# Attention to an MLP on one core: first product reassociated, scores transposed at birth, Silu with 1/beta in w_out, attention woven into the MLP

## Chip, cores and metric

One core of a Trainium2 chip. The metric is the device time of one execution in microseconds (us); most executions of a kernel agree within 0.3%. TensorE is called PE, VectorE DVE, ScalarE ACT, GpSimd POOL. PEld is PE's weight load.

## The reference

Two attentions in a row over 32 packed queries per head, then an MLP with the gate `h * sigmoid(beta h)`:

```python
# q, k, v: (8 batches, 8 heads, 576, 64)   p: (8, 8, 32, 64)
P   = softmax(p @ k.T / 8) @ v            # 32 packed rows per head
out = softmax(q @ P.T / 8) @ P            # A2 @ P
x   = out.transpose(0, 2, 1, 3).reshape(4608, 512)
h   = x @ w_in                            # 512 -> 2048
g   = h * (1 / (1 + exp(-beta * h)))      # beta per column of h
y   = g @ w_out                           # 2048 -> 512, f32
```

## The kernel before

It runs in two stages. Attention goes by groups of four heads, two groups side by side, and fills a resident `xT`; the MLP then goes over nine blocks of 512 tokens. Scores of the second attention are born with tokens on partitions, normalised there, and transposed back chunk by chunk. The code is cut (`# ...`).

```python
def _attn_quad(...):
    # ... k, v, q arrive in 256 B runs, are cast on ACT, transposed on PE, exp, P (p_pack)
    for c, sz in enumerate(SIZES):                    # 128 tokens each
        s2ps = ps_sc.tile([128, 128], f32, ...)
        # ... 4 small matmuls: scores of 4 heads
        nc.scalar.activation(e2t[0:sz, :], s2ps[0:sz, :], EXP, scale=SCALE)
        nc.vector.tensor_reduce(z2[0:sz, :], ...)     # row sums, reciprocal, spread: 3 DVE steps
        nc.vector.tensor_tensor(a2t[0:sz, :], e2t[0:sz, :], rz2e[0:sz, :], MULT)
        _tp(nc, a2c_ps[:, 0:sz], a2t[0:sz, :], identr[:sz, :sz])
        nc.vector.tensor_copy(A2_sb[:, 128 * c : 128 * c + sz], a2c_ps[:, 0:sz])
    for pi in range(2):
        # ... OU_ps = p_pack.T @ A2 (x, transposed), 8 matmuls on 32x64 tiles
        nc.scalar.copy(xT[:, 2 * m + pi, b * S : (b + 1) * S], OU_ps[:, :])

def _mlp_block(...):
    for ft in range(16):
        for kt in range(4):                           # contract 512
            _mm(nc, h_ps[:], w_in_bf[:, kt, ...], xT[:, kt, ...], ...)
        nc.scalar.activation(th[:], h_ps[:], TANH, scale=beta_half[:, ft : ft + 1])
        nc.vector.scalar_tensor_tensor(g_all[:, ft, :], th[:], 1.0, h_ps[:], ADD, MULT)
    # ... 4 x 16 matmuls o_ps = g.T @ w_out, out = 0.5 * o_ps
```

The softmax here doesn't subtract the row's maximum and nothing guards it: scores larger than these inputs give would overflow.

## Time and profile before

| | us | where it is read |
|---|---|---|
| time, median | 526.19 (525.47 to 527.4) | its first three runs |
| attention | 269 | first matmul of h_ps |
| MLP | 249 | 18 blocks of 13.81 in the chain |
| PE, ACT, DVE busy | 424, 255, 218 | busy totals |

The main views are shown and read in the prediction below. One more belongs here, because two of the change's parts aim at it. These are rows of the costliest groups: line, engine, operation, output and inputs, count, then busy us and mean ns of one, then the idle time before them and what ended it.

```profile
L254 DVE SCALAR_TENSOR_TENSOR g_all<-th,h_ps 128x512 bf16<-128x512 bf16 x144 | 99.0, 687 | 142.0 <-ACT th L253 142.0
L38 PE MATMUL h_ps<-xT,w_in_bf 128*128 128x512 bf16 x576 | 128.5, 384 | 0.0
L38 PE MATMUL o_ps<-w_out_bf,g_all 128*128 128x512 bf16 x576 | 125.8, 379 | 0.0
L253 ACT ACTIVATE th<-h_ps,beta_half 128x512 bf16<-128x512 f32 x144 | 98.9, 687 | 28.1 <-PE h_ps L38 28.1
```

The gate costs ACT and DVE 0.69 us each per block of 512 columns, while PE needs 4 x 0.216 = 0.86 us to make the block. So Silu in place of Tanh and a DVE step saves busy time that was hidden; by these figures it would not move the MLP stage by itself.

### The profile page before, as it was taken

Reading aid. Unit: us, or ns where it says so; the run is one execution under the profiler, and the core shown is the slowest. Engines: PE = TensorE matmul, PEld = TensorE weight load, DVE = VectorE, ACT = ScalarE, POOL = GpSimd, SP = SyncE. Lnnn points to the kernel's source line nnn. Section 1 sums busy time; section 2 is a strip of 40 time slices with the busy share of each in tenths; the row PEclk is TensorE's granted clock in tenths of the full one; section 3 lists DMA queues with packets and bytes.
Section 4 is the critical chain, followed back from the end, with each engine's and each line's share of the span. In section 5 each row is a group of like instructions: output and inputs, shape, how many; then the busy total and the mean of one; then the engine's idle time right before and its main releaser. Section 6 shows DMA issues by size and latency. Waiting matters only on the chain.

```text
span 525.3 us, 7290 instructions
## 1 busy us (share of the span) xinstructions
PE 423.9 (81%) x2608; PEld 210.9 (40%) x2608; DVE 217.7 (41%) x722; ACT 254.6 (48%) x517; POOL 18.1 (3%) x26
## 2 busy tenths in 40 slices
PE   0175387868676686667689999999999999999997
PEld 0043154434344353433424444444444444444443
DVE  0047055563726255371637070716253433425260
ACT  1344456556473635637237271727363545445361
POOL 3312300000000000000000000000000000000000
PEclk9999999999999999999999999999999999999999
DMA  8997888888875360000000101010111101010102
GB/s 257 301 210 191 242 190 186 181 194 190 186 171 117 87 149 1 2 1 0 1 1 2 60 21 60 21 58 23 40 42 41 41 20 61 21 61 21 60 1 80
DMA packets 126900, 47.15 MB, mean 90 GB/s; under 512 B 119696, under 2 KB 119696, under 8 KB 126352
## 3 DMA queue, kind: packets, MB, share of 16 engines
q1 hardware_dynamic: 121920, 38.29, 29.1%
q10 hardware_dynamic: 4944, 8.40, 4.7%
q8 instruction: 20, 0.33, 0.3%
q14 instruction: 16, 0.13, 0.1%
HBM read 37.23 MB, written 9.44 MB: 89 GB/s over the span
## 4 chain that ended last, share of the span: by engine, by line
PE 59%; issue 12%; ACT 10%; DVE 7%; DMA 7%; SPq 3%; POOL 1%; ACTq 0%
PE h_ps L38 24%; PE o_ps L38 24%; DMA wout<-in_moe_w_out_dram 4%; SPq L63 3%; PE OU_ps L38 3%; DMA v_quad<-in_v_dram 2%; ACT kT_p L86 2%; DVE z L202 2%; PE kT_ps L44 2%; DVE A_sb L219 2%; PE a2c_ps L44 2%; ACT k_bf L71 2%; DVE rz2e L211 1%; ACT xT L235 1%; PE E1T_ps L44 1%
## 5 line engine op out<-in xcount | busy, mean ns | idle before, releaser
L254 DVE SCALAR_TENSOR_TENSOR g_all<-th,h_ps 128x512 bf16<-128x512 bf16 x144 | 99.0, 687 | 142.0 <-ACT th L253 142.0
L38 PE MATMUL h_ps<-xT,w_in_bf 128*128 128x512 bf16 x576 | 128.5, 384 | 0.0
L38 PE MATMUL o_ps<-w_out_bf,g_all 128*128 128x512 bf16 x576 | 125.8, 379 | 0.0
L253 ACT ACTIVATE th<-h_ps,beta_half 128x512 bf16<-128x512 f32 x144 | 98.9, 687 | 28.1 <-PE h_ps L38 28.1
L38 PEld LDWEIGHTS <-w_in_bf 128*128 128x128 bf16 x576 | 56.5, 99 | 69.8 <-issue 3.4
L38 PEld LDWEIGHTS <-g_all 128*128 128x128 bf16 x576 | 56.4, 98 | 67.9
L266 ACT ACTIVATE o_sb<-o_ps 128x512 f32<-128x512 f32 x36 | 21.5, 597 | 102.5 <-PE o_ps L38 102.5
L200 ACT ACTIVATE e2t<-s_ps 128x128 bf16<-128x128 f32 (+1 forms) x80 | 19.8, 273 | 87.6 <-issue 51.4
L44 PE MATMUL kT_ps<-identr,k_bf 128*128 128x128 bf16 (+1 forms) x160 | 24.6, 291 | 40.7 <-ACT k_bf L71 33.1
L38 PE MATMUL OU_ps<-A_sb,p_pack 32*64 32x64 bf16 (+1 forms) x128 | 29.2, 431 | 11.7 <-ACT xT L235 8.4
L44 PE MATMUL a2c_ps<-identr,a2t 128*128 128x128 bf16 (+1 forms) x80 | 19.5, 277 | 22.2 <-DVE a2t L216 21.4
L44 PEld LDWEIGHTS <-k_bf 128*128 128x128 bf16 (+1 forms) x160 | 14.3, 123 | 54.4 <-ACT k_bf L71 36.5
L128 DVE TENSOR_TENSOR Z<-Z1a,Z1b 128x1 f32<-128x1 f32 x16 | 2.4, 151 | 70.3 <-ACT E_sb L126 70.3
L159 DVE COPY qT_h<-qT_ps 64x576 bf16<-64x576 bf16 x64 | 29.1, 454 | 5.3 <-PE qT_ps L44 4.0
L38 PE MATMUL Pun_ps<-v_bf,E1T_sb 128*32 128x64 bf16 (+1 forms) x320 | 31.2, 238 | 0.0
L235 ACT CAST xT<-OU_ps 128x576 bf16<-128x576 f32 x32 | 20.4, 639 | 22.0 <-PE OU_ps L38 22.0
L44 PE MATMUL qT_ps<-identr,q_bf 128*128 128x128 bf16 (+1 forms) x160 | 23.6, 292 | 5.4 <-ACT q_bf L134 5.4
L38 PE MATMUL s_ps<-p_packT,qT_h 64*128 64x32 bf16 (+1 forms) x320 | 20.7, 191 | 6.7 <-ACT e2t L200 3.9
L38 PEld LDWEIGHTS <-E1T_sb 128*32 128x32 bf16 (+1 forms) x320 | 20.2, 113 | 9.9
L44 PEld LDWEIGHTS <-a2t 128*128 128x128 bf16 (+1 forms) x80 | 8.3, 103 | 38.9 <-DVE a2t L216 30.0
L38 PEld LDWEIGHTS <-qT_h 64*128 64x128 bf16 (+1 forms) x320 | 17.0, 110 | 14.5 <-issue 8.3
L86 ACT COPY kT_p<-kT_ps 128x576 bf16<-128x576 bf16 x32 | 19.8, 642 | 5.4 <-POOL w_out_bf L306 2.8
(44 smaller groups left out, 295.6 us busy)
## 6 DMA issues: line engine op xcount, KB each, us to landing
out_dram<-o_sb SPq DMA_DIRECT2D x36, 256.0 KB, 2.0
k_quad<-in_k_dram SPq DMA_DIRECT2D x64, 128.0 KB, 2.8
v_quad<-in_v_dram SPq DMA_DIRECT2D x64, 128.0 KB, 2.8
q_quad<-in_q_dram SPq DMA_DIRECT2D x64, 128.0 KB, 2.8
win<-in_moe_w_in_dram ACTq DMA_DIRECT2D x4, 1024.0 KB, 6.8
wout<-in_moe_w_out_dram ACTq DMA_DIRECT2D x16, 256.0 KB, 3.5
k_quad<-in_k_dram SPq DMA_DIRECT2D x16, 64.0 KB, 3.1
v_quad<-in_v_dram SPq DMA_DIRECT2D x16, 64.0 KB, 2.7
```

Source lines behind the costliest of these rows:

```text
L38: return nc.tensor.matmul(out, lhsT, rhs, start=start, stop=stop, tile_position=tile_position, skip_group_check=True)
L44: return nc.tensor.matmul(out, in_, ident, is_transpose=True, tile_position=tile_position, skip_group_check=True)
L63: nc.sync.dma_start(dst[0:sz, c, :].rearrange("p (h d) -> p h d", d=D), src[b, h4, 128 * c : 128 * c + sz, :].rearrange("h p d -> p h d"),)
L71: nc.scalar.copy(tbf[:, 0:4, :], t32[:, 0:4, :])
L86: nc.scalar.copy(tsb[:], tps[:])
L159: nc.vector.tensor_copy(qh[:, :], tps[64 * li : 64 * li + 64, :])
L200: nc.scalar.activation(e2t[0:sz, :], s2ps[0:sz, :], EXP, scale=SCALE)
L202: nc.vector.tensor_reduce(z2[0:sz, :], e2t[0:sz, :].rearrange("p (h j) -> p h j", j=NP), axis=mybir.AxisListType.X, op=ADD,)
L235: nc.scalar.copy(xT[:, 2 * m + pi, b * S : (b + 1) * S], OU_ps[:, :])
L253: nc.scalar.activation(th[:], h_ps[:], TANH, scale=beta_half[:, ft : ft + 1])
L254: nc.vector.scalar_tensor_tensor(g_all[:, ft, :], th[:], 1.0, h_ps[:], ADD, MULT)
L266: nc.scalar.mul(o_sb[:], o_ps[:], 0.5)
```

## The change

The intent is to give PE fewer columns and no pauses:

- **Reassociation.** `(A2 @ P) @ w_in = A2 @ (P @ w_in)`. Per batch, W = P @ w_in has 8 heads x 32 = 256 rows, so h contracts 256, not 512.
- **Transposed scores.** Scores are computed with keys on partitions; sums over keys become matmuls with ones. No transpose of weights is left.
- **Silu.** `h * sigmoid(beta h) = silu(beta h) / beta`: beta is multiplied into W, 1/beta into w_out.
- **Loads.** Token 4p+t lies on partition p, so a partition reads 4 tokens, 1 KB at a time.
- **Weaving.** One loop over batches; phase i holds the first product of batch i, the attention of batch i+1 and the second product of batch i-1, in a hand-set order.

The kernel is written anew; this is its core, cut.

```diff
+    def fused_w(self, b, n):                       # W = P @ w_in, 512 columns at a time
+        for c in range(NC):
+            for r in range(2):
+                self.mm(ps[32*c:32*c+32, r, :], pp[64*r:64*r+64, c, :],
+                        self.w_in_bf[64*r:64*r+64, c, cols], pos=(64*r, 32*c))
+        self.nc.vector.tensor_tensor(W[:, :, cols], ps, beta_bc[:, cols]..., ALU.mult)
+    def mlp_main(self, b, ft):
+        for r in range(2):                         # contract 256 in place of 512
+            self.mm(ps[:], W[:, r, 128*ft:128*ft+128], A[:, r, 0:SM], start=(r == 0), stop=(r == 1))
+        self.nc.scalar.activation(self.g[b][:, ft, :], ps[:], AF.Silu)
+    def cast_w_out(self, n, t):
+        for i in range(4):
+            self.nc.gpsimd.tensor_scalar_mul(self.w_out_bf[:, ft, :], t[:, i, :], self.rbeta[:, ft:ft+1])
+    def run(self):                                 # ... batch 0: load, attention, W, with w_in by quarters
+        o2 = self.load_w_out(2); self.cast_w_out(1, o1)      # two staging buffers for w_in and w_out
+        o3 = self.load_w_out(3); self.cast_w_out(2, o2); self.cast_w_out(3, o3)
+        for x in "kqv": self.load(1, x)
+        for x in "kqv": self.cast(1, x, pcopy)     # pcopy: POOL
+        # ... loads of batch 2
+        for i in range(B): self.phase(i)
+    def phase(self, i):                            # main(ft, n): h of one ft, then n matmuls of second(i-1)
+        main(0, 2); attn("transpose_main", nb, "k"); main(1, 2); attn("transpose_main", nb, "q")
+        # ...
+        attn("exp_set"); attn("scores1", nb); attn("silu_set"); fill(14)
+        main(6, 2); attn("packed", nb)
+        # ...
+        attn("exp_set"); attn("scores2", nb); fill(8); attn("norm2", nb); attn("silu_set"); fill(8)
+        # ... fused_w 0 to 3 among main 10 to 15, remainder of 64 tokens, rest of second(i-1)
```

## The prediction

> **What bounds the kernel now.** I read the page first: busy totals and the 40 slices. They show a kernel in two halves.
>
> ```profile
> span 525.3 us, 7290 instructions
> PE 423.9 (81%) x2608; PEld 210.9 (40%) x2608; DVE 217.7 (41%) x722; ACT 254.6 (48%) x517; POOL 18.1 (3%) x26
> PE   0175387868676686667689999999999999999997
> DVE  0047055563726255371637070716253433425260
> ACT  1344456556473635637237271727363545445361
> DMA  8997888888875360000000101010111101010102
> ...
> PE 59%; issue 12%; ACT 10%; DVE 7%; DMA 7%; SPq 3%; POOL 1%; ACTq 0%
> ```
>
> From about slice 21 on (13 us each) PE is full. Before it no engine is: attention has PE, DVE and ACT at 4 to 8 tenths, and DMA full only for 13 slices. The chain of waits says the same: the matmuls of h_ps and o_ps carry 24% each, and the rest is a ladder of small pieces on every engine. Busy time by stretch puts the border near 269 us (columns: stretch, length, busy us and instructions of PE, PEld, DVE, ACT, POOL, then clock, DMA share, GB/s):
>
> ```profile
> 0.00:40.00 40.00, 12.70 (x114) 7.76 (x114) 6.61 (x22) 13.53 (x29) 10.72 (x14) 1.00 0.93 255
> 40.00:200.00 160.00, 110.56 (x948) 63.49 (x945) 78.76 (x386) 85.34 (x219) 7.34 (x12) 1.00 0.73 170
> 200.00:269.00 69.00, 47.94 (x391) 26.41 (x389) 33.38 (x170) 33.50 (x88) 0.00 (x0) 1.00 0.00 1
> ```
>
> Even at 200:269, where DMA is idle, PE is busy 69%: attention is bound by latency between engines, not by data. The second half is bound by PE issue: in the chain in order of time every 64 matmuls of 512 columns take 13.81 us, 216 ns each, 18 such blocks = 249 us.
>
> The timeline gives what small matmuls cost:
>
> ```profile
> 300.68 13.81 PE h_ps L38 x64
> 314.49 13.81 PE o_ps L38 x64
> ...
> 181.60 1.48 PE L44 MATMUL kT_ps<-identr,k_bf 128*128 128x128 bf16 x10 [2.13 <-ACT k_bf L71]
> 183.21 0.45 PE L38 MATMUL S1a_ps<-kT_p,pT_p 64*32 64x320 bf16 x4
> 183.81 0.40 PE L38 MATMUL S1b_ps<-kT_p,pT_p 64*32 64x256 bf16 x4
> ```
>
> Four matmuls on four 64x32 tiles of the array take 0.45 us together, where one lasts 0.453 us: they run at the same time. In the starts of single instructions the full-height transposes follow each other in 107 ns, and each change to a 64-row one and back adds about 0.25 us.
>
> **What the Trainium skill says.** "TensorE: Matmul & The Clock Gate", Part 3 (Packing small matmuls): matmuls on different row and column tiles run concurrently; the S1a row agrees. "TensorEngine Tiling (Array Packing)", Key Properties: changing the tiling mode drains the engine; the 0.25 us agrees in kind. "ScalarE: Activation LUTs", What ACT_TABLE_LOAD costs: 1283 ns, plus a drain of 1380 ns, per switch to another set. The trace has one load, 1283 ns, with the next ACT instruction starting right at its end, so I count 1.3 us and keep the drain as a risk. "DMA: Bandwidth & Descriptors", Why small descriptors are slow: small ones waste the engines. Here 119,696 of 126,900 packets are under 512 B; the busy first 20 us moved 269 GB/s with the weights' large rows among them, the next stretches 183 to 227 at 81 to 88% share.
>
> **The change, part by part.** Per batch of 576 tokens:
>
> (1) First product. Before: 576 matmuls of 512 columns, 124 us, plus A2@P (OU_ps, 29 us busy) and its copies (xT, 20 us of ACT). After: W = P@w_in costs 4 groups of 8 tiled matmuls (64x32, 512 columns); if all 8 run at once a group is 0.22 us plus 0.25 us of mode change. Then h = A2@W contracts 256 rather than 512: 32 matmuls = 6.9 us, and 32 of 64 columns for the remainder, about 1 us at 30 ns. So 8 x (6.9 + 1.0 + 1.9) = 78 us in place of over 124.
>
> (2) Second product: 36 tiles x 16 x 0.216 = 124 us, unchanged. This is the floor that remains.
>
> (3) Scores born transposed: E1T and a2c transposes (80 matmuls each), the row sums, the rz2e copies and 320 + 320 small matmuls go. Left per batch: 36 transposes of 107 ns = 3.9 us; scores1 0.6; packed 1.2; scores2 0.3; norm2 0.5; two more mode changes 0.5. About 7 us.
>
> (4) Weaving. Attention for batch b+1 is laid in program order among the MLP matmuls of b and the second product of b-1. PE per phase: main 6.9 + remainder 1.0 + W 1.9 + attention 7.0 + second product 13.8 (4 tiles) or 17.3 (5 tiles) = 30.6 or 34.1.
>
> (5) ACT per phase: 18 Silu at about 0.60 (the row o_sb, 128x512 from PSUM with an immediate scale, took 597 ns; Tanh with a pointer scale 687) = 10.8; Exp and Ln 6.3 (about 0.2 + 0.85 ns per column, from 597 ns at 512 and 1045 at 1024); 4 table loads 5.1. Sum 22, below PE. DVE: 2 copies of 2048 bf16 (425 ns at 512, 223 at 128, so 1.2 each), 4 products of 1024 f32 (687 at 512, so 1.2 each), A2 1.3, outputs 2.7, the rest 1.5: 13. POOL: 3 casts at about 2.1 (1892 ns at 2048) = 6.4. DMA: 3.5 MB of load and 1.2 MB of store in over 30 us, with 1 KB runs: idle two thirds of the time. So PE alone binds, and this time in all stages.
>
> I walked one phase in program order to see where PE waits. Table load after the sixth Silu at 9.4 us, Exp until 12.3, Silu table back at 13.6; PE meets packed at 13.4 and main 8 at 15.8, both just ready. Second switch 17.7 to 19.0, E2 ready at 20.3, where the fill of 8 has just run out at 20.1; Ln and Exp run under 14 fills. Sum 32.3 or 35.8: 1.7 us of small waits over the pure PE sum.
>
> (6) Ends. At the start nothing overlaps: k, p, v, q and the first quarter of w_in are 5.1 MB, 21 us at 0.27 MB/us. Then the first attention and the quarters of w_in alternate: only two staging buffers, so quarter 3 is issued after quarter 1 is cast; W is complete at about 40 us. w_out goes through the same two buffers until about 53 us with scaling on POOL to 55; the loads of batch 1 stand behind it in the queue and land to 63 us, and their casts stand behind on POOL. Phase 0 needs those, starts late and has no second product to fill with: Silu at 0.6 and four table loads bind, some 20 us after q arrives. Phase 0 ends at about 85 us. Phase 7 has no attention: 6.9 + 1.0 + 13.8 = 22. Then 80 bare matmuls 17.3, copy and store 3.2.
>
> Sum: 85 + 3 x 32.3 + 3 x 35.8 + 22 + 20.5 = 332; 4 us for cold-clock stretches and semaphores I did not see: **336 us**.
>
> **Rivals.** (a) Table switching binds: with the 1.38 us drain, each pair of switches delays Silu and Exp by 2.8 us where fills run out; 3 to 5 us in 7 phases, so 355 to 370. For it: the page. Against: the trace's one load shows no gap behind it, and fills of 14 and 8 cover much. (b) The tiled groups of 8 do not run all at once (two row groups on one column group were seen only as a pair on different columns): 4 at once costs 0.2 us x 5 groups x 8 = 9 us; fully serial 1.5 x 5 x 8 = 60 us, near 395. Against serial: the S1a row. (c) The start is worse: single-buffered loads, small staging, f32 matmuls for beta, slow strided casts on POOL: plus 10 to 20 us. Or better, if 1 KB runs reach 0.33 MB/us: minus 8. (d) Nothing gained because PE was 81% busy already: the 424 us count overlapping latencies (384 ns for a matmul issued every 216), so busy is no measure of work; I give this no weight.
>
> **Range and chances.** Start plus or minus 12, phases minus 1 to plus 4 each, tail firm: 318 to 360. To be slower than 516 us, everything would have to fail together. Faster by over 2%: 0.98; within 2%: 0.01; slower: 0.01.
>
> **What would show it.** Right: from 85 us on PE at 9 tenths in nearly every slice; second product still 216 ns a matmul; phases of 32 and 36 us by turns; W groups of 8 in under 0.6 us; ACT 45 to 60% busy; DMA at 1 to 3 tenths. Wrong: PE gaps of over 1 us before packed, main 8 or z2 in each phase, released by ACT (rival a); W groups over 1 us (b); first output-product matmul after 100 us (c). An ACT or POOL busier than PE would make the whole sum wrong.

## The result, and the profile after

The changed kernel takes 333.15 us (332.07 to 334.49, four runs) against 526.14 us of the kernel before in its runs beside it; the ratio is 0.633 (95% interval 0.631 to 0.635). The output is correct.

First the page: busy totals, the 40 slices (8.3 us each; PEclk is the clock recorded for PE in tenths of full, DMA the busy share of the 16 DMA engines) and the chain of waits by engine.

```profile
span 331.5 us, 5201 instructions
PE 257.6 (78%) x2188; PEld 134.7 (41%) x2225; DVE 120.4 (36%) x155; ACT 167.7 (51%) x242; POOL 77.4 (23%) x69
PE   0297320006659999999999999999999999999994
ACT  1024230000986877587458757862886687443300
POOL 3030008999520520440043005200510000000000
PEclk9999555555969999999999999999999999999999
DMA  8960553599994492097029606912010010111122
...
PE 71%; ACT 7%; POOL 7%; DMA 5%; issue 4%; DVE 4%; DVEq 0%; POOLq 0%
```

PE is full from the thirteenth slice to the end, in one stage now rather than in half the kernel. The other thing to see is the front: PE at zero in the seventh to ninth slice while POOL stands at 8 to 9 tenths.

The busy time by phase says how long each part is. The stretches begin at the first h matmul of each batch; the first two lines are the start, then phases 0, 1, 2, 7 and the tail. Phases 3 and 5 repeat phase 1, phases 4 and 6 repeat phase 2.

```profile
0.00:49.10 49.10, 19.73 (x184) 15.94 (x185) 21.75 (x34) 11.80 (x14) 6.23 (x11) 0.82 0.61 184
49.10:77.50 28.40, 1.09 (x11) 0.17 (x4) 1.23 (x1) 0.60 (x1) 26.58 (x18) 0.50 0.73 229
77.50:103.90 26.40, 19.46 (x196) 10.51 (x200) 10.31 (x12) 19.18 (x29) 11.33 (x11) 0.77 1.08 288
103.90:132.90 29.00, 28.14 (x260) 14.31 (x265) 12.80 (x16) 20.70 (x30) 6.66 (x6) 1.00 0.54 152
132.90:165.20 32.30, 31.33 (x279) 15.71 (x281) 13.46 (x17) 21.36 (x31) 6.66 (x6) 1.00 0.51 151
...
287.80:309.40 21.60, 21.50 (x126) 10.26 (x127) 2.98 (x5) 10.15 (x17) 0.00 (x0) 1.00 0.15 49
309.40:331.50 22.10, 17.38 (x86) 7.80 (x84) 3.94 (x6) 0.60 (x1) 0.00 (x0) 1.00 0.21 72
```

Set these beside the sum of the prediction:

| part | predicted | measured | difference |
|---|---|---|---|
| start and phase 0 | 85 | 103.9 | +18.9 |
| phases 1 to 6 | 3 x 32.3 + 3 x 35.8 = 204.3 | 3 x 29.0 + 3 x 32.3 = 183.9 | -20.4 |
| phase 7 | 22 | 21.6 | -0.4 |
| tail | 20.5 | 22.1 | +1.6 |
| not seen | 4 | | -4 |
| sum | 336 | 331.5 (span) | -4.5 |

So the total came out by luck: two of its terms were off by some 20 us in opposite directions. The experiments ask for the cause of both, and what the large gain is made of.

The late start, in the timeline (start us, length us, instructions, then the idle time before and what ended it):

```profile
50.92 24.65 POOL L412 TENSOR_SCALAR w_out_bf<-w_out,rbeta 128x512 bf16<-128x512 f32 x16 [31.05 <-DMA w_out<-in_moe_w_out_dram]
75.52 1.89 POOL L87 CAST k_bf<-k 128x2048 bf16<-128x2048 f32 x1
77.47 1.89 PE L63 MATMUL kT_ps<-identr,k_bf 128*128 128x128 bf16 x16 [27.30 <-POOL k_bf L87]
```

POOL scales w_out for 24.65 us without a pause, casts k of batch 1 behind it, and PE, idle for 27.30 us, transposes k the moment that cast ends. One scaling lasts 24.7 / 16 = 1.56 us (1563 ns on the page). The same tile's plain cast in the kernel before took 0.61 us, and the prediction's end at 55 us fits that length.

The short phases, in the timeline of PE in phase 2:

```profile
133.67 1.06 PE L63 MATMUL kT_ps<-identr,k_bf 128*128 128x128 bf16 x16
...
147.88 0.44 PE L58 MATMUL s_ps<-qT,pp 64*32 64x512 bf16 x16
148.48 1.68 PE L58 MATMUL o_ps<-w_out_bf,g_main 128*128 128x512 bf16 x7 [0.16 <-issue]
150.76 0.65 PE L58 MATMUL z_ps<-E2T,bones 128*128 128x512 bf16 x4 [0.60 <-ACT E2T L212]
...
153.06 0.41 PE L58 MATMUL w_ps<-w_in_bf,pp 64*32 64x512 bf16 x8
```

Sixteen transposes take 1.06 us from first start to last end; in the single records they start 56 ns apart, where the same instruction at 77.47 takes 107. Eight tiled matmuls of 512 columns end within 0.41 us: all eight run at once. The only waits of PE that the timeline lists in this phase are the two shown, 0.16 and 0.60 us.

### The profile page after: what moved, and what is told of

It reads as the page before. It is cut to its first block, busy times and chain, and to the rows that moved or that the text cites. A ratio compares the mean times of both kernels' runs of the same rounds, so it can differ in the third digit from the quotient of the medians.

```text
span 331.5 us, 5201 instructions
## 1 busy us (share of the span) xinstructions
PE 257.6 (78%) x2188; PEld 134.7 (41%) x2225; DVE 120.4 (36%) x155; ACT 167.7 (51%) x242; POOL 77.4 (23%) x69
## 3 DMA queue, kind: packets, MB, share of 16 engines
q1 hardware_dynamic: 47488, 46.15, 46.8%
## 4 chain that ended last, share of the span: by engine, by line
PE 71%; ACT 7%; POOL 7%; DMA 5%; issue 4%; DVE 4%; DVEq 0%; POOLq 0%
PE o_ps L58 34%; PE h_ps L58 18%; POOL w_out_bf L412 7%; PE w_ps L58 4%; DMA p<-in_p_dram 3%; PE kT_ps L63 3%; PE qT_ps L63 3%; PE pp_ps L58 3%; ACT E2T L212 2%; PE brow_ps L58 2%; ACT g_main L266 2%; DMA w_out<-in_moe_w_out_dram 2%; PE z_ps L58 1%; DVE w_in_bf L400 1%; PE s_ps L58 1%
## 5 line engine op out<-in xcount | busy, mean ns | idle before, releaser
L58 PE MATMUL o_ps<-w_out_bf,g_main 128*128 128x512 bf16 x496 | 131.7, 380 | 1.7 <-issue 0.5
L266 ACT ACTIVATE g_main<-h_ps 128x512 bf16<-128x512 f32 x128 | 75.8, 597 | 99.3 <-PE h_ps L58 89.5
L58 PE MATMUL h_ps<-A2T,W_bf 128*128 128x64 bf16 (+1 forms) x494 | 83.7, 288 | 1.2 <-ACT g_main L266 0.7
L58 PEld LDWEIGHTS <-g_main 128*128 128x128 bf16 x512 | 47.9, 98 | 55.6 <-issue 2.7
L303 DVE COPY o_sb<-o_ps 128x512 f32<-128x512 f32 x36 | 24.9, 692 | 103.8 <-PE o_ps L58 103.8
L58 PEld LDWEIGHTS <-W_bf 128*128 128x128 bf16 x512 | 31.1, 98 | 28.3 <-issue 8.3
L249 DVE TENSOR_TENSOR W_bf<-w_ps,beta_bc 128x1024 bf16<-128x1024 f32 x32 | 38.4, 1221 | 10.0 <-PE w_ps L58 9.1
L412 POOL TENSOR_SCALAR w_out_bf<-w_out,rbeta 128x512 bf16<-128x512 f32 x16 | 24.7, 1563 | 31.1 <-DMA w_out<-in_moe_w_out_dram 31.1
L58 PE MATMUL w_ps<-w_in_bf,pp 64*32 64x512 bf16 x256 | 14.6, 434 | 11.7 <-DVE w_in_bf L400 10.7
L126 ACT ACT_TABLE_LOAD x15 | 19.2, 1283 | 4.8 <-issue 4.6
L129 ACT ACT_TABLE_LOAD x15 | 19.2, 1283 | 0.3
L87 POOL CAST q_bf<-q 128x2048 bf16<-128x2048 f32 x8 | 15.1, 1894 | 15.1 <-DMA q<-in_q_dram 15.1
L87 POOL CAST v_bf<-v 128x2048 bf16<-128x2048 f32 x7 | 13.3, 1893 | 20.3 <-issue 18.5
```

The source lines that it names most:

```text
L58: return self.nc.tensor.matmul(out, lhsT, rhs, start=start, stop=stop, tile_position=pos, skip_group_check=True)
L87: copy(o[:, 0:2048].rearrange("p (t h d) -> p h t d", t=4, h=8), t[:, 0:2048].rearrange("p (h t d) -> p h t d", h=8, t=4),)
L126: self.nc.scalar.preload_act_table_set(EXP_SET)
L129: self.nc.scalar.preload_act_table_set(SILU_SET)
L249: self.nc.vector.tensor_tensor(W[:, :, cols], ps, self.beta_bc[:, cols].unsqueeze(1).to_broadcast([128, 2, 512]), ALU.mult,)
L266: self.nc.scalar.activation(self.g[b][:, ft, :], ps[:], AF.Silu)
```

## The experiments

Eleven kernels were run. Those timed over three rounds have four runs, all fast; the others are one look each, of unknown state, and are used only for differences of many per cent or for their traces. All are correct but two.

**1. Is the scaling on POOL what holds the start? (e_cast_only)** The factor is left out, so the result is wrong.

```diff
-            self.nc.gpsimd.tensor_scalar_mul(self.w_out_bf[:, ft, :], t[:, i, :], self.rbeta[:, ft : ft + 1])
+            self.nc.gpsimd.tensor_copy(self.w_out_bf[:, ft, :], t[:, i, :])
```

> The 1/beta factor is left out of w_out on purpose (wrong result): the 16 GpSimd multiplications become plain casts. Theory 1 (the late start is the GpSimd scaling, 16 x 1563 ns in front of the casts of batch 1): the casts take about 0.61 us each, the staging buffers come free sooner, the k cast of batch 1 starts near 66 us instead of 75.5, the total falls by 8 to 12 us to about 323; phases 1 to 6 stay 29.0 and 32.3 us. Rival (the transfers of w_out and of batch 1 bind, GpSimd only looks busy): the k cast moves by under 3 us and the total stays over 330.

Measured: 324.94 us (323.80 to 325.49), 8.2 us less. POOL's timeline in this kernel:

```profile
50.54 2.30 POOL L412 CAST w_out_bf<-w_out 128x512 bf16<-128x512 f32 x4 [30.50 <-DMA w_out<-in_moe_w_out_dram]
...
62.01 2.30 POOL L412 CAST w_out_bf<-w_out 128x512 bf16<-128x512 f32 x4 [1.58 <-DMA w_out<-in_moe_w_out_dram]
65.97 1.90 POOL L87 CAST k_bf<-k 128x2048 bf16<-128x2048 f32 x1 [1.66 <-DMA k<-in_k_dram]
```

Four casts take 2.30 us where four scalings took 4 x 1.56 = 6.2, the k cast starts at 65.97 instead of 75.52, and now it waits for DMA: the engine is no longer the limit, the place of the load in the queue is. Phases 1 to 6 keep their 29.0 and 32.3 us. Theory 1 holds, but it is worth 8.2 of the 18.9 us by which the start was late: without the scaling w_out is still ready only at 64.3 us.

**2. Does the start need w_out at all? (e_order)** Batch 1 is loaded and cast ahead of the second half of w_in and of w_out. w_out is first read in phase 1.

```diff
         self.fused_w(0, 0)
         self.scores2(0)
+        for x in "kqv": self.load(1, x)
+        for x in "kqv": self.cast(1, x, pcopy)
         w2 = self.load_w_in(2)
 # ...
         self.cast_w_out(3, o3)
-        for x in "kqv": self.load(1, x)
-        for x in "kqv": self.cast(1, x, pcopy)
```

> Batch 1 is loaded and cast before quarters 2 and 3 of w_in and before w_out; nothing else changes. Theory 1 (phase 0 waits only for its place in the DMA queue and on GpSimd): phase 0 starts at about 50 us instead of 77 with no wait, phase 1 starts near 77 to 80, when the last w_out part has been scaled; total about 308 (303 to 314). Rival (the DMA engines are the limit of the start): w_in is pushed back by what batch 1 moves, about 12 us, phase 0 starts near 61 and the total is about 320 or more.

Measured: 308.06 us (307.73 to 309.30), correct, ratio to the kernel before 0.585 (0.583 to 0.587). It beats both kernels. The stretch of phase 0 in this kernel:

```profile
51.00:78.60 27.60, 21.11 (x197) 10.69 (x193) 11.60 (x13) 19.56 (x29) 25.96 (x17) 0.81 0.72 222
```

POOL still spends its 25 us on w_out, but beside phase 0, not ahead of it. From the first Silu of a phase to that of the next, phase 0 fell from 54.3 to 27.8 us; W came 1.9 us later and phase 1 grew by 0.7 because batch 2 is cast late. The sum, -26.6 + 1.9 + 0.7 = -24.0, is the change of the span. So an order, in the DMA queue and on POOL, was worth more than the whole first difference of the table.

**3. Do the table loads cost? (e_one_table)** Silu becomes Exp (wrong), so that one table set serves.

```diff
-        self.nc.scalar.activation(self.g[b][:, ft, :], ps[:], AF.Silu)
+        self.nc.scalar.activation(self.g[b][:, ft, :], ps[:], AF.Exp)
     def silu_set(self):
-        self.nc.scalar.preload_act_table_set(SILU_SET)
+        pass                       # and exp_set only once
```

> Silu is replaced by Exp on purpose (wrong result), so that one table set serves all: 29 of 30 table loads of 1.28 us go, all else stays. Theory (loads hide behind PE work except in phase 0): phases 1 to 6 shorten by at most 0.7 us each, the wait of z_ps for E2T, phase 0 by 3 to 5; total 324 to 329. Rival (table switching binds each phase): phases shorten by 2.6 us or more each, total 315 or less.

Measured: 326.13 us (325.10 to 326.49), 7.0 less. Phases 1 to 6 shorten by 0.76 us each, a little more than the 0.7 allowed for; phase 0, where nothing fills, by 2.8. Removing four loads of 1.28 us per phase thus returns 0.76 of 5.1 us: the rest is hidden behind other work. Rival (a) of the prediction falls. The loads show no drain either: in the trace of the changed kernel a load that follows a Silu directly starts 17 or 18 ns after its end, and Exp 11 or 12 ns after the end of the load.

**4. What is the weave worth? (e_unwoven)** The same instructions, with the attention of the next batch as one block behind the MLP.

```diff
-        main(0, 2); attn("transpose_main", nb, "k"); main(1, 2); ...
+        for ft in range(16): main(ft, 4)
+        self.mlp_rem(i, 0); self.mlp_rem(i, 1)
+        for _ in w2: pass
+        attn("transpose_main", nb, "k"); attn("transpose_main", nb, "q"); ...   # all of attention
```

> The attention of the next batch stands as one block behind the MLP of the phase instead of among its matmuls; same instructions. Theory (weaving hides a latency chain of some 18 us of which only 7 us is PE work): phases 1 to 6 grow by about 11 us each to 40 and 43, phase 0 gains some 5, total about 395 (375 to 410), and the transposes fall back to about 107 ns each where PE was idle before. Rival (the fewer and larger instructions carry the gain and order matters little): total within 15 us of 333.

Measured: 399.62 us, 66.5 more. Phases that took 29.0 and 32.3 take 40.9 and 44.4. One long phase:

```profile
137.10:181.50 44.40, 35.65 (x285) 17.85 (x281) 13.61 (x18) 18.20 (x28) 6.60 (x6) 0.85 0.39 111
```

The clock column is 0.85: within each phase the trace has the clock at half for 10 to 14 us (130.8 to 141.1, 171.8 to 185.4). One detail of the expectation missed: the transposes kept 56 ns. They come right behind the dense second product, where the record still says full clock; what ran slow was the W groups at the end of the latency chain and the first matmuls of the next phase. So the weave is worth two things at once, hidden latency and a clock that stays up (1.00 in the woven phases 1 to 7); how the 66.5 us divides between them was not measured.

**5. What is the reassociation worth? (e_noreassoc)** x = A2 @ P is formed again and h contracts 512; beta then goes into w_in once, at its cast on VectorE, and all else stays.

```diff
-    # fused_w: W = P @ w_in, 4 groups of 8 tiled matmuls, times beta
+    # one transpose of P, then per 128 rows of x:
+            self.mm(ps[h, lo:hi], ppT[k, h], A[k, r, lo:hi], pos=(32 * c, 64 * r))
+            self.nc.vector.tensor_copy(xT[:, c, :], ps[:, 0:S])
-        for r in range(2):
+        for r in range(4):        # mlp_main and mlp_rem over w_in * beta and xT
```

> The reassociation alone is undone: x = A2@P is formed per batch (8 tiled matmuls of 512 and 8 of 64 columns, 4 copies of 576 columns on VectorE) and h contracts 512 again, with beta folded into w_in once; weaving, transposed scores, Silu and loads stay. Theory (phases are bound by PE issue): per phase 32 more matmuls of 512 at 0.216 = +6.9, 32 more of 64 columns = +0.9, W groups -1.7, x +1.5, so phases 1 to 6 go from 29.0 and 32.3 to about 36.6 and 39.9; phase 7 +7.8, phase 0 +4; total about 390 (380 to 400). Rival (forming W per batch costs as many matmuls as it saves): within 15 us of 333.

Measured: 386.18 us, 53.0 more. Phases take 36.0 and 39.45, so 7.0 and 7.1 more, against 7.6 expected; 32 more matmuls at 0.216 are 6.9 of it. Phases are bound by PE issue, and the rival falls.

**6. Do the two gains add? (e_both_undone)** Both edits at once.

> Reassociation and weaving both undone (h contracts 512 over x; attention as one block behind each MLP phase). Theory (the two gains are independent: fewer PE columns, and latency hidden): they add, 333 + 53 + 66 = 452 (442 to 462); the 75 us that are left to 526 belong to the rest: scores born transposed, larger instructions, one pass. Rival (they overlap, a longer MLP hides more): under 435.

Measured: 459.63 us. They add nearly: 53.0 + 66.5 would make 452.6, and 7 more was found. The gain of 193 us divides so:

| step | us |
|---|---|
| before to both undone: transposed scores, larger instructions, one loop | 526.9 to 459.6 = 67 |
| reassociation (unwoven, or woven) | 60 or 53 |
| weaving (over x, or over W) | 73 or 66 |

Three of these totals are single; the steps are far above the 0.3% within which most runs agree. The first row was not divided further: what the transposed scores, Silu, the single loop and the clock each carry in it is not shown.

**7. Do the 1 KB runs matter? (e_rows256)** Back to one token per partition row, 256 B at a time.

```diff
-        nc.sync.dma_start(..., src[b, :, 0:SM, :].rearrange("h (p t) d -> p h (t d)", p=128))
+        for i in range(4):
+            nc.sync.dma_start(..., src[b, :, 128 * i : 128 * i + 128, :].rearrange("h p d -> p h d"))
-                rows = ... .rearrange("(p t) n -> p t n", t=4)
+                rows = ... .rearrange("(t p) n -> p t n", t=4)
```

> The 4 tokens per partition are undone: k, v and q come in runs of 256 B (4 DMAs per tensor in place of 1), the output rows follow. Theory (loads are hidden in phases 1 to 6 and GpSimd binds the start): phases 1 to 6 stay 29.0 and 32.3 us, the start is 4 to 8 us later because q of batch 0 and the casts of batch 1 come later; total 337 to 342. Rival (the longer runs carry a large part of the gain, DMA becomes the limit): phases 1 to 4 grow, total over 350.

Measured: 333.96 us (332.33 to 334.20), the same; the expected 4 to 8 us did not come. The packets changed, first the changed kernel's line and then this one's:

```profile
DMA packets 49607, 47.01 MB, mean 142 GB/s; under 512 B 16288, under 2 KB 40880, under 8 KB 49584
```

```profile
DMA packets 124488, 47.02 MB, mean 142 GB/s; under 512 B 115744, under 2 KB 115760, under 8 KB 124464
```

Two things cancelled what I had expected. p landed earlier, so its cast began at 7.2 us and not at 10.5, and batch 1 waited for POOL in both kernels (first cast of k at 73.8 and 75.5). This part of the change carries nothing in the total here. The waste of small packets is real but hidden: for the same 46.15 MB the main queue takes 63.0% of the 16 engines' span instead of 46.8%.

**8. Is 107 ns the transpose, or the clock? (e_order_warm)** In e_order PE waits while W groups 2 and 3 of batch 0 become ready. Useless matmuls fill that wait.

```diff
         ps = self.att("w_ps")...
+        if b == 0 and n >= 2:
+            for _ in range(16 if n == 2 else 12):
+                self.mm(ps[:, 0, :], self.identr[:], dummy)      # 512 columns, overwritten after
```

> The version with batch 1 loaded before w_out, and in it 28 useless matmuls of 512 columns in front of the W groups 2 and 3 of batch 0, where PE waits anyway. Theory (the 107 ns of a transpose is the array at half clock after idling, not a property of transposes or of the instruction mix): the 16 k transposes of phase 0 follow each other in 56 ns rather than 107, the first h matmuls in 216 rather than 427, total 2 to 3 us below the same version without them (308). Rival (transposes are slow unless embedded in other work, or the useless matmuls delay W): 107 ns stays, total the same or up to 3 us more.

Measured: 308.44 us (307.61 to 309.39), so nothing gained on 308.06. But the transposes of phase 0 answer the question:

```profile
52.56 0.60 PE L58 MATMUL h_ps<-A2T,W_bf 128*128 128x512 bf16 x2
53.01 1.06 PE L63 MATMUL kT_ps<-identr,k_bf 128*128 128x128 bf16 x16
```

1.06 us for the sixteen, where the same row reads 1.91 in e_order and 1.89 in the changed kernel. The cause is the clock: it is recorded as full from 48.0 to 61.7 us here, and as half from 31.6 to 82.8 us in the changed kernel, whose sixteen start at 77.47. The time was not saved because the useless matmuls, the first of them at half clock themselves, held W back by as much: phase 0 took 1.8 us less and began 1.1 us later, and phase 1 then waited 0.8 us longer for POOL.

**9. The same question in the kernel before (e_before_3banks, e_before_warm).** The control frees a PSUM bank; the second run adds 576 useless matmuls, each fed by data of its own step so that the scheduler cannot pull them forward.

```diff
-    name="ps_b1", bufs=4, space=PSUM
+    name="ps_b1", bufs=3, space=PSUM
+    # e_before_warm only, at every step of _attn_quad:
+        _mm(nc, fill[:, 0:w], identr[:], src, start=True, stop=True)    # 36 per group of four heads
```

> Control: the kernel before with 3 instead of 4 rotating PSUM tiles in attention, one bank freed. All theories: attention ends 0 to 15 us later than 269 us, the MLP is unchanged, total 526 to 545; transposes still 107 ns apart.

> The control, with 36 useless matmuls per group of four heads (9,216 columns) spread over the attention stage: 61 us more PE issue time at full clock, 123 at half clock. Theory (attention of the kernel before runs on an array at half clock because PE pauses too often, though the record of granted clock says 1.00): transposes follow each other in 56 ns in most of the stage, the first h matmuls in 216 ns, and the useless work costs little: total within minus 25 to plus 25 us of the control. Rival (107 ns is what a transpose costs amid tiled matmuls): 107 ns stays and the total grows by 50 us or more.

Measured: the control 528.20 us, attention ending at 271 us; with the useless work 553.41, attention ending at 298. Of 92 pairs of neighbouring k transposes that the control's trace holds, 60 start 106 to 107 ns apart and none 56; with the useless work 39 of 94 start 55 to 56 ns apart, 11 more 63 to 67, and 37 still 106 to 107, and every h matmul runs at 216 from the first.

The record of the clock agrees: all 39 lie where it says full, and of the 37 slow ones 27 lie where it says half and 10 ahead of its first entry. So the pace follows the clock in this kernel too. But only 105 of the stage's 298 us are recorded at full clock, not most of it, and the total grew by 25.2 us, just outside the range that the theory allowed. Filling with useless work does not pay here; the weave fills with useful work. What the half clock cost the kernel before stays open.

**10. A further step (e_order_head).** On top of e_order_warm, the f32 matmuls that spread beta and the cast of k are issued ahead of the preparation of p.

```diff
-        self.prepare_p(); self.prepare_beta(); w = self.load_w_in(0); self.cast(0, "k", vcopy)
+        self.prepare_beta(); self.cast(0, "k", vcopy); self.prepare_p(); w = self.load_w_in(0)
```

> As e_order_warm, and the beta rows and the cast of k are issued before the preparation of p, so that 7 us of f32 matmuls run while the data is still on its way. Theory (the f32 matmuls stand on the path of the start): scores1 of batch 0 starts 4 to 5 us sooner than 28.9 us and phase 0 as well; total about 301 (299 to 304). Rival (the arrival of q and w_in binds the start): under 2 us of gain over e_order_warm.

Measured: 305.80 us (304.24 to 307.28), correct, ratio 0.580 (0.578 to 0.583): the fastest, 2.6 us below e_order_warm where 7 were expected. scores1 did start 3.8 us sooner than in e_order_warm, at 24.9 us, and the first W group 4.6 us sooner, at 32.8. But the second cast of w_in then took 2.7 us where it takes 1.2 in e_order_warm, with POOL casting v at the same time; the first useless matmuls took 6.5 instead of 5.9 us; and phase 1 lost 0.6 us to late casts. Neither theory had the size.

## Why the prediction was right or wrong

**What bounds the kernel before:** right that the MLP is PE issue; that attention is latency fits, but it missed that attention ran at half clock, and no run separates the two there. It took the clock column, 1.00, as it stood. The clock record in the trace has only one change before the end: to full, at 275.4 us. Before it nothing is recorded, and the page fills the gap with full speed. The timeline shows the change:

```profile
269.04 1.89 PE L38 MATMUL h_ps<-xT,w_in_bf 128*128 128x512 bf16 x4
...
271.47 2.31 PE L38 MATMUL h_ps<-xT,w_in_bf 128*128 128x512 bf16 x5
```

Four matmuls in 1.89 us and five in 2.31. In the single records they start 0.427 us apart, against 0.216 from 275.5 us on. Experiments 8 and 9 show that the 107 ns between k transposes have the same reason.

**Part (1), first product:** right. h took 32 x 0.216 and the remainder about 0.9; a W group costs about 0.44 us with its change of tiling mode (153.06 to 153.41, and 0.09 ahead of it), so 1.7 per phase against 1.9. Undoing it cost 7.0 to 7.1 us per phase.

**Part (2), second product unchanged:** right. Phases with five output tiles are 3.3 us longer than those with four, 16 x 0.216 = 3.45.

**Part (3), "36 transposes of 107 ns = 3.9 us":** wrong size. They take 36 x 0.056 = 2.0. The mechanism, PE issue time of attention, was right; the term was read off an array at half clock. This is 1.9 of the 3.3 us by which each phase was over-estimated.

**Part (4) and the walk:** right in kind, wrong in size. PE is idle for under 1 us per phase (29.00 - 28.14, 32.30 - 31.33), not 1.7, and the one wait of note, z2 behind Exp, was named. Of the 3.3 us, 1.9 are the transposes, about 0.8 the waits and 0.2 the W groups; some 0.4 us per phase remain that I did not assign.

**Part (5), other engines:** ACT 20.3 to 21.4 against 22, DVE 13 against 13, POOL 6.66 against 6.4: right. DMA "idle two thirds of the time" was wrong for phases 1 to 4, where its share is 0.51 to 0.56; it binds in none of these phases, where PE is idle for under 1 us.

**Part (6), "with scaling on POOL to 55":** the step that failed. Its end fits 16 scalings at the 0.61 us of a cast; they took 1.56 each, to 75.6 us, and e_cast_only shows that this cost 8.2 us. W was also complete at about 49 and not at 40 us, which set w_out and batch 1 back as well. The f32 matmuls for beta, unsized in the prediction, took 7.2 us on PE; but having them earlier (e_order_head) brought the first h matmul only 2.6 us forward, so the cause of these 9 us is shown only in part. The chain itself, w_out ahead of batch 1 in the queue and on POOL, was named, and e_order shows that it held phase 0: with the order changed, phase 0 runs as soon as W is complete.

**The rivals:** (a) table switching and (b) serial tiles fell. (c) a worse start came true in size, nearly at the upper end of its 10 to 20 us, and its sign, the first output-product matmul after 100 us, was seen; of its causes the casts on POOL took 1.89 us, as long as expected, and what held the start was the order and the scaling, which it does not list.

**That the total came so close was luck.** With the phases at their measured length the forecast would have been 336 - 20.4 = 316 us, below its own range and 17 us under the measured time. Three sums also don't come out: 5.1 MB at 0.27 MB/us is 19 us and not 21; the 4.7 MB of a phase at that rate are 17 us, over half of it, which is not "idle two thirds"; and 12 us and six times 4 on top of 336 make 372, not 360.

## What to carry to other kernels

Ask what each engine at the start of a pipeline must finish before the first full phase may begin, and put the loads and casts of the second batch ahead of weights that are needed only later: here that was worth 25 of 333 us and no new instruction. When latency chains alternate with dense matmuls, weave them: here that hid the chain, kept the clock up, and was worth 66 us. And before a duration of a small matmul is carried over from a trace, check the array's clock by the pace of a large one beside it, not by the clock column alone.

## What the Trainium skill lacked or had wrong

- "TensorE: Matmul & The Clock Gate", Part 4 (PE-mode transpose), says that the full clock "doesn't engage" for transposes. Behind other dense work they run at it: 56 ns for 128 columns, 107 when the array is at half clock.
- The same page, Part 1, describes the change between half and full clock and warns that its recorded events can be unreliable, but no page says that a stage ahead of the first recorded change has no clock in the trace: the profile of the kernel before shows 1.00 up to 275.4 us, though ahead of that a matmul of 512 columns took 0.427 us and a k transpose 107 ns.
- "ScalarE: Activation LUTs", What ACT_TABLE_LOAD costs, adds a drain of 1380 ns to each switch. A load starts 17 or 18 ns after the Silu ahead of it, Exp 11 or 12 ns after the end of the load of 1283 ns, and removing 29 loads returned 7.0 us, not 29 x 2.66 = 77 us; a drain that other work hides cannot be told from none by the total, but none shows on ACT.
- "GPSIMD Engine Reference", 4.1 Engine selection, calls operations with one input "roughly line-rate". A cast of 128x512 from f32 took 0.61 us on POOL, a multiplication by a per-partition factor 1.56 us.
- "TensorEngine Tiling (Array Packing)", Key Properties, names the drain at a change of mode but no size: a group of eight 64x32 tiles with 512 columns and its change cost about 0.44 us, 0.22 of it the columns.
